# A decode kernel on one core: the tile context is closed behind the first three loads instead of around the whole program

## The chip, the cores and the metric

The kernel runs on 1 core of one Trainium2 chip. The metric is the device time of one execution in microseconds (us); less is better.

## The reference

One token (x, 512 values) goes through two branches, and a scalar gate mixes them. All numbers are float32.

```python
g = sigmoid((x * gate_w).sum(-1))
q = (x @ wq)                                  # 32 heads of 128
scores = q . k_cache * 128 ** -0.5            # 8 kv heads, 32768 positions, 4 query heads share one
a = softmax(scores) @ v_cache @ wo            # 4096 -> 512
b = (silu(x @ w1) * (x @ w3)) @ w2            # 512 -> 1792 -> 512
return g * a + (1 - g) * b
```

The K and V caches are 8 x 32768 x 128 floats each, 134 MB; with the weights the kernel reads 296 MB from HBM.

## The kernel before, in words

The program is written out by hand: it allocates its own semaphores (42 of them, in `_program`) and places every wait itself. The tile framework only wraps it. `kernel` opens a tile context at L485; `tile_gated_mix_decode_kernel` opens a critical section in it at L27, whose synchronizing engine is ScalarE (the profile's ACT), and runs the whole of `_program` inside. Instructions which the section emits at its entry and exit carry L27, those of the context L485. The start of every program, with four small constants and a barrier of all engines, carries L476.

Three SBUF buffers of 8 MB (64 KB in each of 128 partitions), ra, rb and rc, take all large loads. SyncE (SP in the profile) issues them, in this order: wq into rc (L118), w1 and w3 into the two parts of rb (L119, L120), then the two halves of the first K part into ra (L121, L122). Next it waits until the matmuls with w1 and w3 have freed rb (L123) and loads the second K part into rb (L124). Then a loop over the 8 kv heads loads each further half of K into ra or rb, and each half of V into rc, as TensorE releases the buffer (L127 to L137). At the end it loads the last V halves into ra and rb, wo into rc (L146) and w2 into ra (L152).

ScalarE issues three small transfers at the start: x (L155), the gate weights (L156) and, once VectorE has cleared a row, that zero row to the output (L162). At the end it issues the result (L460). Its semaphore l_out counts 16 for each of the two output transfers.

The work at the start: GpSimd (POOL) builds an identity and clears buffers (L166 to L173), VectorE (DVE) clears and reduces (L160 to L177), TensorE (PE) spreads x over the partitions (L187) and multiplies the gate (L196) as soon as x and the gate weights are there, then the query from wq (L202) and the two branches of the feed-forward from w1 and w3 (L229). ScalarE applies the sigmoids (L209, which needs a table load, and L241).

In the loop of 8 heads VectorE transposes K in 32 x 32 blocks (L342), TensorE multiplies (L271), VectorE and TensorE find the maxima, ScalarE exponentiates (L386), and TensorE multiplies with V of the head before (L285). Behind the loop come the last head, the projection with wo (L421), w2 (L428, L438), and four copies of a piece of the result each (L456). The program ends with GpSimd's wait for both output transfers (L461); then the section and the context are left.

Of the kernel before, what the change touches and what calls it, by code (L numbers as in the profile page):

```python
# [3 lines left out]
F32 = mybir.dt.float32  # L4
# [5 lines left out]
P = 128  # L10
# [13 lines left out]

@with_exitstack
def kernel(ctx, tc, x, k_cache, v_cache, wq, wo, w1, w3, w2, gate_w, out):
    with tc.tile_critical(sync_engine=mybir.EngineType.Activation, no_gpsimd_drain=True):  # L27
        _program(tc.nc, x, k_cache, v_cache, wq, wo, w1, w3, w2, gate_w, out)


def _program(nc, x, k_cache, v_cache, wq, wo, w1, w3, w2, gate_w, out):
    pe, dve, act, pool, sp = nc.tensor, nc.vector, nc.scalar, nc.gpsimd, nc.sync
    _, HKV, S, DH = k_cache.shape
    D = x.shape[-1]
    F = w1.shape[1]
    HQ = wq.shape[1] // DH
    REP = HQ // HKV
    NC = D // P
# [4 lines left out]
    W = NK * DH  # L43
    assert DH == P and D == 4 * P and REP == 4 and HKV == 8 and NK == 128 and F == FR * P

    def sb(name, *shape):
        return nc.alloc_sbuf_tensor(name, [P, *shape], F32).ap()

    def token(name):
        return nc.alloc_semaphore(name)  # L50

    def count(name):
        return Count(nc, name)


    ra, rb, rc = sb("ra", W), sb("rb", W), sb("rc", W)

    ident, ones, fold, dmask = sb("ident", P), sb("ones", P), sb("fold", 32), sb("dmask", 4)
    xp = sb("xp", NC, 32)
# [30 lines left out]
    pq = [bank(3), bank(4)]  # L90


    l_x, l_q = token("l_x"), token("l_q")
    l_a, l_a2, l_b, l_c = token("l_a"), token("l_a2"), token("l_b"), token("l_c")
    l_w1, l_w3 = token("l_w1"), token("l_w3")
    l_v = [token(f"l_v{i}") for i in range(2)]
    l_wo = [token(f"l_wo{i}") for i in range(2)]
    l_w2 = [token(f"l_w2{i}") for i in range(4)]
    l_out = token("l_out")

    c_q, c_k, c_v, c_e = (count(n) for n in ("c_q", "c_k", "c_v", "c_e"))
    c_nm, c_act, c_pool, done = token("c_nm"), count("c_act"), count("c_pool"), count("done")
# [12 lines left out]
    kd = k_cache.rearrange("a h (p m n) d -> (a h) m p (n d)", p=P, m=2, n=NK)  # L115
    vd = v_cache.rearrange("a h (r p n) d -> (a h) r p (n d)", r=2, p=P, n=NK)
    half = W // 2
    sp.dma_start(rc, wq.rearrange("(p c) n -> p (c n)", c=NC)).then_inc(l_q, 16)  # L118
    sp.dma_start(rb[:, 0:NC * F], w1.rearrange("(p c) f -> p (c f)", c=NC)).then_inc(l_w1, 16)  # L119
    sp.dma_start(rb[:, NC * F:2 * NC * F], w3.rearrange("(p c) f -> p (c f)", c=NC)).then_inc(l_w3, 16)  # L120
    sp.dma_start(ra[:, 0:half], kd[0, 0][:, 0:half]).then_inc(l_a, 16)  # L121
    sp.dma_start(ra[:, half:W], kd[0, 0][:, half:W]).then_inc(l_a2, 16)  # L122
    sp.wait_ge(c_e.sem, 2)  # L123
# [27 lines left out]
    for i in range(4):  # L151
# [17 lines left out]
        out=ident, in_=ident, compare_op=ALU.not_equal, fill=1.0, base=0, pattern=[[-1, P]], channel_multiplier=1,  # L169
# [256 lines left out]
    for k in range(W2[1]):  # L426
        t = k % 4
        i = pe.matmul(  # L428
            acc[32 * t:32 * t + 32, :], htp[:, k, :], w2t[:, k, :], start=False, stop=(k >= W2[1] - 4),
            skip_group_check=True,  # L430
        )
# [22 lines left out]
    for j in range(4):  # L454
        copy = act.copy if j % 2 else dve.tensor_copy
        i = copy(row[:, j * P:(j + 1) * P], pb[32 * j:32 * j + 1, 0:P])  # L456
# [1 line left out]
            done.by(i)  # L458
    act.wait_ge(done.sem, done.n)
    act.dma_start(od, row).then_inc(l_out, 16)  # L460
    c_pool.by(pool.wait_ge(l_out, 32))  # L461


# [26 lines left out]
```

## Time and profile before

| | us |
|---|---|
| runs shown | 693.97, 694.00, 694.11 |
| their median | 694.0 |
| the profiled execution's own time | 694.02 |
| its span, from the first to the last instruction | 691.9 |
| TensorE busy in the span | 368.2 |
| VectorE busy in the span | 307.0 |

The kernel moved 296.35 MB at a mean of 428 GB/s in the span.

How to read it: times in the profile count from the first instruction of the execution. "Busy" does not count register, branch, semaphore and DMA-issuing instructions; they belong to an engine's sequencer, which the rows mark with a q behind the engine (SPq, ACTq, POOLq, and PEldq for TensorE's). A row of the timeline has start, duration, engine, line, operation, what it writes and reads, and in brackets the idle time before it with what ended that. A row of a single source line has the count, the shortest, median and longest duration in ns, and the starts of the first and the last. "DMA to landing" is the time from issue to the arrival of the last byte. A row of the windows has the window, its length, the busy time of each engine with its instruction count (PE, PEld, DVE, ACT, POOL), the clock granted to TensorE, the mean share of the 16 DMA engines, and GB/s. The digits behind "DMA" on the page are that share in 40 equal slices of the span, in tenths.

### The profile page before, as it was taken

Reading aid. Unit: us, or ns where it says so; the run is one execution under the profiler, and the core shown is the slowest. Engines: PE = TensorE matmul, PEld = TensorE weight load, DVE = VectorE, ACT = ScalarE, POOL = GpSimd, SP = SyncE. Lnnn points to the kernel's source line nnn. Section 1 sums busy time; section 2 is a strip of 40 time slices with the busy share of each in tenths; the row PEclk is TensorE's granted clock in tenths of the full one; section 3 lists DMA queues with packets and bytes.
Section 4 is the critical chain, followed back from the end, with each engine's and each line's share of the span. In section 5 each row is a group of like instructions: output and inputs, shape, how many; then the busy total and the mean of one; then the engine's idle time right before and its main releaser. Section 6 shows DMA issues by size and latency. Waiting matters only on the chain. (4 is left out here: it accounts for less than half of the span.)

```text
span 691.9 us, 6738 instructions
## 1 busy us (share of the span) xinstructions
PE 368.2 (53%) x2952; PEld 107.5 (16%) x2952; DVE 307.0 (44%) x194; ACT 41.6 (6%) x111; POOL 7.0 (1%) x41
## 2 busy tenths in 40 slices
PE   1636255467463734466573735466463734466567
PEld 1100011103010121103010211103010211103122
DVE  1019378291725447091825446191816356181000
ACT  0020011002000010002000010001000010001000
POOL 0000000000000000000000000000000000000000
PEclk9975598868686977779577967888786966798678
DMA  9999999999999999999999999999999999999996
GB/s 383 421 439 454 424 429 425 447 447 424 425 432 432 436 447 436 424 424 432 432 440 451 428 424 428 436 428 443 447 424 424 432 432 436 447 436 424 424 423 291
DMA packets 6078, 296.35 MB, mean 428 GB/s; under 512 B 691, under 2 KB 691, under 8 KB 950
## 3 DMA queue, kind: packets, MB, share of 16 engines
q1 hardware_dynamic: 6048, 296.23, 99.2%
q8 instruction: 6, 0.10, 0.1%
q14 instruction: 2, 0.02, 0.0%
q10 hardware_dynamic: 22, 0.01, 0.0%
HBM read 296.23 MB, written 0.00 MB: 428 GB/s over the span
## 5 line engine op out<-in xcount | busy, mean ns | idle before, releaser
L342 DVE STREAM_TRANSPOSE rb<-rb 128x2048 f32<-128x2048 f32 x64 | 141.8, 2275 | 150.3 <-DVEq L112 150.3
L342 DVE STREAM_TRANSPOSE ra<-ra 128x2048 f32<-128x2048 f32 x64 | 141.4, 2275 | 43.6 <-DVEq L112 43.6
L271 PE MATMUL psum<-rb,winbuf 128*32 128x512 f32 x512 | 88.2, 766 | 130.2 <-PEq L112 130.2
L285 PE MATMUL psum<-rc,prob 128*32 128x512 f32 x896 | 111.2, 653 | 42.5 <-PEq L112 42.5
L271 PE MATMUL psum<-ra,winbuf 128*32 128x512 f32 x512 | 85.2, 764 | 86.7 <-PEq L112 86.7
L285 PEld LDWEIGHTS psum<-rc,prob 128*32 128x32 f32 x896 | 33.5, 120 | 115.5 <-issue 115.3
L366 DVE TENSOR_REDUCE mx<-psum 128x4 f32<-128x1024 f32 x8 | 9.8, 1224 | 81.6 <-DVEq L112 81.6
L271 PEld LDWEIGHTS psum<-rb,winbuf 128*32 128x32 f32 x512 | 13.1, 120 | 203.7 <-issue 203.7
L380 ACT COPY sbuf<-psum 128x512 f32<-128x512 f32 x16 | 9.8, 616 | 477.0 <-PE psum L271 477.0
L271 PEld LDWEIGHTS psum<-ra,winbuf 128*32 128x32 f32 x512 | 14.7, 121 | 150.1 <-issue 150.1
L386 ACT ACTIVATE prob<-psum,nm 128x256 f32<-128x256 f32 x32 | 18.8, 694 | 39.6 <-DVE nm L374 39.6
L295 PE MATMUL psum<-ident,sbuf 128*64 128x64 f32 x512 | 16.7, 223 | 0.8 <-PEq L112 0.8
L295 PEld LDWEIGHTS psum<-ident,sbuf 128*64 128x64 f32 x512 | 15.6, 138 | 7.6 <-issue 7.6
L347 DVE SCALAR_TENSOR_TENSOR otall<-psum,gate,recip 128x4 f32 (+1 forms) x8 | 1.7, 213 | 33.1 <-DVEq L112 33.1
L202 PE MATMUL psum<-rc,xp 128*32 128x512 f32 x64 | 9.8, 783 | 9.2 <-DMA rc<-in_A_wq_dram 9.2
L285 PE MATMUL psum<-rb,prob 128*32 128x512 f32 x64 | 8.4, 684 | 9.8 <-DMA rb<-in_A_v_cache_dram 9.8
L421 PE MATMUL psum<-rc,oq 128*32 128x512 f32 x64 | 10.7, 829 | 2.5 <-DMA rc<-in_A_wo_dram 2.1
L258 POOL COPY winbuf<-winraw 32x16 f32<-32x16 f32 x32 | 6.1, 189 | 537.2 <-PE psum L271 499.6
L285 PE MATMUL psum<-ra,prob 128*32 128x512 f32 x64 | 9.5, 761 | 3.7 <-DMA ra<-in_A_v_cache_dram 3.7
L229 PE MATMUL psum<-rb,xp 128*32 128x448 f32 x64 | 8.4, 683 | 5.6 <-DMA rb<-in_B_w_dram 5.6
L214 DVE STREAM_TRANSPOSE rc<-psum 128x512 f32<-128x512 f32 x2 | 1.3, 696 | 18.7 <-PE psum L202 18.7
L305 PE MATMUL psum<-fold,ob 128*128 128x4 f32 x64 | 8.4, 255 | 0.8 <-PEq L112 0.8
(62 smaller groups left out, 80.6 us busy)
## 6 DMA issues: line engine op xcount, KB each, us to landing
ra<-in_A_k_cache_dram SPq DMA_DIRECT2D x2, 4096.0 KB, 53.3
rc<-in_A_wo_dram SPq DMA_DIRECT2D x2, 4096.0 KB, 45.9
rb<-in_B_w_dram SPq DMA_DIRECT2D x2, 3584.0 KB, 34.7
ra<-in_B_w_dram SPq DMA_DIRECT2D x1, 1536.0 KB, 32.8
ra<-in_B_w_dram SPq DMA_DIRECT2D x1, 1024.0 KB, 35.0
ra<-in_B_w_dram SPq DMA_DIRECT2D x1, 768.0 KB, 36.3
ra<-in_B_w_dram SPq DMA_DIRECT2D x1, 256.0 KB, 36.5
rc<-in_A_v_cache_dram SPq DMA_DIRECT2D x14, 30.6
```

Of the source, the lines that this page charges most:

```text
L202: m = pe.matmul(pq[b][32 * j:32 * j + 32, :], xp[:, c, :], rc[:, o:o + REP * DH], start=(c == 0), stop=(c == NC - 1),)
L229: i = pe.matmul(ps[32 * j:32 * j + 32, 0:FJ], xp[:, c, :], rb[:, o:o + FJ], start=(c == 0), stop=(c == NC - 1))
L258: pool.tensor_copy(winbuf[32 * r:32 * r + 32, 16:144].rearrange("p (c k) -> p c k", k=32)[:, :, 4 * r:4 * r + REP], winraw[32 * r:32 * r + ...
L271: i = pe.matmul(s_ps[m][32 * g:32 * g + 32, :], winbuf[:, w:w + 32], region.rearrange("p (n c i) -> p c n i", c=4, i=32)[:, c, n:n + 16], ...
L285: i = pe.matmul(o_ps[32 * t:32 * t + 32, :], prob[:, w:w + 32], region[:, n * DH:(n + 4) * DH], start=(r == 0 and g == 0 and f == 0), stop ...
L295: i = pe.matmul(pf[64 * s:64 * s + 64, 64 * a:64 * a + 64], sbuf[:, a].rearrange("p i m -> p (i m)"), ident.rearrange("p (gf r s q) -> p s ...
L305: i = pe.matmul(mb[:, 0:REP], ob[:, b * P:(b + 1) * P], fold[:, 4 * b:4 * b + 4], start=(b == 0), stop=(b == 3))
L342: dve.transpose(part[:, c], part[:, c]).then_inc(t_tr, 1)
L366: dve.tensor_reduce(mx, pf.rearrange("p (a q) -> p q a", q=REP), axis=AX.X, op=ALU.max).then_inc(t_mx, 1)
L380: act.copy(sbuf[:, :, :, m], s_ps[m].rearrange("p (n i) -> p n i", i=32)).then_inc(t_ev, 1)
L386: act.activation(prob[:, 0:1024].rearrange("p (a n q) -> p n a q", a=16, q=REP)[:, :, :, q], pf.rearrange("p (n a q) -> p n a q", n=16, q= ...
L421: pe.matmul(acc[32 * t:32 * t + 32, :], oq[:, k:k + 32], rc[:, k * D:(k + 1) * D], start=(k < 4), stop=False, skip_group_check=True,)
```

## The change

`tile_gated_mix_decode_kernel` no longer opens a critical section. It allocates rb and rc and three semaphores, issues the loads of wq, w1 and w3 from SyncE inside the context, marked so that the framework puts no semaphores of its own on them, closes and compiles the context by hand, and then runs `_program`, which follows the context without a section. `_program` allocates only ra (behind rb and rc now), and its SyncE part begins with the first K part. At the end GpSimd still waits for both output transfers, and then clears all semaphores of the program. The `with` at L485 that opens the context is left as it is.

```diff
 def tile_gated_mix_decode_kernel(ctx, tc, x, k_cache, v_cache, wq, wo, w1, w3, w2, gate_w, out):
-    with tc.tile_critical(sync_engine=mybir.EngineType.Activation, no_gpsimd_drain=True):
-        _program(tc.nc, x, k_cache, v_cache, wq, wo, w1, w3, w2, gate_w, out)
-
-
-def _program(nc, x, k_cache, v_cache, wq, wo, w1, w3, w2, gate_w, out):
+    nc = tc.nc
+    rb, rc = (nc.alloc_sbuf_tensor(n, [P, 16384], F32).ap() for n in ("rb", "rc"))
+    l_q, l_w1, l_w3 = (nc.alloc_semaphore(n) for n in ("l_q", "l_w1", "l_w3"))
+    loads = [(rc, wq, l_q)]
+    n = w1.shape[0] * w1.shape[1] // P
+    loads += [(rb[:, i * n:(i + 1) * n], w, sem) for i, (w, sem) in enumerate(((w1, l_w1), (w3, l_w3)))]
+    for to, w, sem in loads:
+        i = nc.sync.dma_start(to, w.rearrange("(p c) n -> p (c n)", p=P)).then_inc(sem, 16)
+
+        tc.no_tile_sem_insts.add(i.ins.name)
+    tc.close()
+    tc.compile()
+    _program(nc, rb, rc, l_q, l_w1, l_w3, x, k_cache, v_cache, wq, wo, w1, w3, w2, gate_w, out)
+
+
+def _program(nc, rb, rc, l_q, l_w1, l_w3, x, k_cache, v_cache, wq, wo, w1, w3, w2, gate_w, out):
...
+    before = nc.snapshot_sems()
+
+
+    ra = sb("ra", W)
...
-    sp.dma_start(rc, wq.rearrange("(p c) n -> p (c n)", c=NC)).then_inc(l_q, 16)
-    sp.dma_start(rb[:, 0:NC * F], w1.rearrange("(p c) f -> p (c f)", c=NC)).then_inc(l_w1, 16)
-    sp.dma_start(rb[:, NC * F:2 * NC * F], w3.rearrange("(p c) f -> p (c f)", c=NC)).then_inc(l_w3, 16)
     sp.dma_start(ra[:, 0:half], kd[0, 0][:, 0:half]).then_inc(l_a, 16)
...
     act.dma_start(od, row).then_inc(l_out, 16)
-    c_pool.by(pool.wait_ge(l_out, 32))
+    pool.wait_ge(l_out, 32)
+    nc.clear_and_free_semaphores([l_q, l_w1, l_w3, *nc.allocated_since(before)])
```

More of the change, by code (lines that the diff above doesn't have):

```diff
@@ L53, in count @@
         return Count(nc, name)
-    ra, rb, rc = sb("ra", W), sb("rb", W), sb("rc", W)
+    before = nc.snapshot_sems()
+    ra = sb("ra", W)
     ident, ones, fold, dmask = sb("ident", P), sb("ones", P), sb("fold", 32), sb("dmask", 4)
@@ L90, in _program @@
     pq = [bank(3), bank(4)]
-    l_x, l_q = token("l_x"), token("l_q")
+    l_x = token("l_x")
     l_a, l_a2, l_b, l_c = token("l_a"), token("l_a2"), token("l_b"), token("l_c")
-    l_w1, l_w3 = token("l_w1"), token("l_w3")
     l_v = [token(f"l_v{i}") for i in range(2)]
```

## The prediction, made before the result was known

> **What bounds the kernel now.** I read the page first (span, slices, DMA queues), then the windows by stage, then the beginning and the end of the timeline, and last the rows of the lines that emit the section's own instructions (L27) and the context's (L485).
>
> ```profile
> span 691.9 us, 6738 instructions
> PE 368.2 (53%) x2952; PEld 107.5 (16%) x2952; DVE 307.0 (44%) x194; ACT 41.6 (6%) x111; POOL 7.0 (1%) x41
> DMA  9999999999999999999999999999999999999996
> q1 hardware_dynamic: 6048, 296.23, 99.2%
> 60.00:672.00 612.00, 327.30 (x2642) 94.33 (x2642) 290.96 (x173) 34.68 (x89) 5.30 (x28) 0.78 1.00 433
> ```
>
> The reader is to see that the 16 DMA engines are the bound: the q1 row gives their share by the SyncE queue's packets as 99.2% of the span, and in the window from 60 to 672 us the DMA share is 1.00. The busiest engine, TensorE, is at 53%. A change that touches no transfer can therefore act in three places only: when the stream starts, whether it ever runs dry, and what is left after its last byte.
>
> The beginning and the start of the loop:
>
> ```profile
> 0.92 0.37 SPq L118 DMA_DIRECT2D rc<-in_A_wq_dram  x1
> 0.97 0.53 ACTq L155 DMA_DIRECT2D ob<-in_A_x_dram  x1
> 1.54 0.73 ACTq L156 DMA_DIRECT2D prob<-in_gate_w_dram  x1
> 1.78 0.22 POOL L173 MEMSET winbuf<- 128x144 f32 x1
> 1.82 0.42 SPq L120 DMA_DIRECT2D rb<-in_B_w_dram  x1
> 2.08 0.27 DVE L177 TENSOR_REDUCE dmask<-ident 128x4 f32<-128x128 f32 x1
> 2.29 0.53 SPq L121 DMA_DIRECT2D ra<-in_A_k_cache_dram  x1
> 2.31 0.43 ACTq L162 DMA_DIRECT2D out_dram<-sbuf  x1
> 2.77 1.28 ACT L209 ACT_TABLE_LOAD   x1 [2.77 <-DVE ones L165]
> 10.74 1.94 PEld L187 LDWEIGHTS psum<-ones,ob 1*128 1x128 f32 x8 [10.74 <-DMA prob<-in_gate_w_dram]
> 13.11 0.55 PE L196 MATMUL psum<-gsm,ones 1*128 1x1 f32 x2 [0.35 <-PEq L112]
> 22.82 9.83 PE L202 MATMUL psum<-rc,xp 128*32 128x512 f32 x64 [9.15 <-DMA rc<-in_A_wq_dram]
> 46.64 0.33 SPq L124 DMA_DIRECT2D rb<-in_A_k_cache_dram  x1
> ```
>
> SyncE issues five loads within 2.5 us and then has nothing to do until 46.64, when both w matmuls have freed rb. TensorE waits 9.15 us for wq after all its small work is done. The head of the program is thus loose on every engine; only the first issue, at 0.92, is tight.
>
> The end, after the last matmul, with the rows of L27, L461 and L485 (count, ns of one, first to last start):
>
> ```profile
> 689.85 0.21 ACTq L460 DMA_DIRECT2D out_dram<-prob  x1
> L461 POOLq EVENT_SEMAPHORE  x1: 17/17/17, 691.0 to 691.0; - x1
> L27 POOLq NOP  x1: 13/13/13, 691.1 to 691.1; - x1
> L27 ACTq DRAIN  x1: 158/158/158, 690.2 to 690.2; - x1
> L485 POOLq DRAIN  x3: 34/41/64, 691.1 to 691.6; - x3
> L485 POOLq EVENT_SEMAPHORE  x4: 17/17/17, 691.2 to 691.7; - x4
> L485 POOLq EVENT_SEMAPHORE_RANGE_CLEAR  x1: 71/71/71, 691.5 to 691.5; - x1
> L485 SPq EVENT_SEMAPHORE  x4: 17/22/73, 690.2 to 691.8; - x4
> L485 DVEq EVENT_SEMAPHORE  x2: 21/21/21, 691.4 to 691.8; - x2
> L485 ACTq EVENT_SEMAPHORE  x2: 17/17/17, 691.4 to 691.8; - x2
> L485 PEldq EVENT_SEMAPHORE  x2: 51/51/51, 691.4 to 691.8; - x2
> ```
>
> GpSimd sees the landed result at 691.0 (L461). What follows, up to 691.9, computes nothing: GpSimd leaves the section (L27), gathers all engines, releases them at 691.4 (the first of the two that each of VectorE, ScalarE and TensorE has), clears a range of semaphores at 691.5 and releases all again at 691.8. That is 0.9 us, with rounding 0.8 to 0.9, on the path that sets the end. The profiled execution took 694.02 us, so 2.1 us lie around the span; it stands 0.02 above the median of the runs (694.0).
>
> **The change part by part.**
>
> *The tail.* Gone from the end are the exit from the section and the context's gathering, release, clearing, gathering and release. Added behind L461 is a clearing by GpSimd alone. I read it as the same range clear (71 ns), perhaps with one drain ahead (at most 64 ns). Nine GpSimd instructions lie from the NOP at 691.1 to the last release at 691.7, counting it and the three kinds of L485 rows: 1 + 3 + 4 + 1. They take some 0.08 us apiece, waits included. So: one step of 0.08 to the first new instruction, 0.071 for the clear, one more 0.08 if a drain stands ahead, together 0.15 to 0.25 us in place of 0.8 to 0.9. The gain is 0.55 to 0.75 us; I take 0.65. No other engine's end can come later: the last matter for ACT, the issue of the result, starts at 689.85, and its wait for all others is gone.
>
> *The first load.* These are the rows that stand between the start barrier and the first load:
>
> ```profile
> L476 SPq EVENT_SEMAPHORE  x1: 17/17/17, 0.7 to 0.7; - x1
> L485 SPq COMPARE_BRANCH  x1: 33/33/33, 0.8 to 0.8; - x1
> L27 ACTq NOP  x2: 14/16/18, 0.7 to 691.1; - x2
> ```
>
> SyncE is released by the start barrier at 0.7, branches at 0.8 when ScalarE's NOP of the section (0.7) has signalled, and issues at 0.92. In the changed kernel the loads stand in the context itself, so they don't wait for ScalarE. If the branch stays, only the handshake goes, which is under 0.1 us; if it goes too, the issue comes right behind the release, at about 0.7, 0.2 us earlier. Nothing suggests a later issue, so the bounds are 0 and 0.25 us. I take 0.1, since a branch into the context's block is likely to stay. The whole stream moves by this, and the end with it, since the window rows show no stretch in which another engine sets the pace.
>
> *What is moved to the head.* Behind the three loads every engine now goes through the closing sequence, 0.7 to 0.9 us by the rows of the tail. SyncE's third issue ends at 1.82 + 0.42 = 2.24 now, at 2.1 if all shifts by 0.1. So the program proper starts at about 2.9 to 3.0 us on all engines, where ScalarE and SyncE stood at 0.97 (L155) and 2.29 (L121). Queue by queue:
>
> - SyncE's two loads of the K cache (L121, L122) are issued 0.6 to 0.8 us later. They wait behind the three weight loads anyway:
>
> ```profile
> L120 SPq DMA_DIRECT2D rb<-in_B_w_dram x1: 424/424/424, 1.8 to 1.8; - x1
> DMA to landing us min/median/max: 39.4/39.4/39.4
> L121 SPq DMA_DIRECT2D ra<-in_A_k_cache_dram x1: 530/530/530, 2.3 to 2.3; - x1
> DMA to landing us min/median/max: 48.7/48.7/48.7
> L122 SPq DMA_DIRECT2D ra<-in_A_k_cache_dram x1: 521/521/521, 2.9 to 2.9; - x1
> DMA to landing us min/median/max: 57.8/57.8/57.8
> ```
>
>   The third load lands at 1.8 + 39.4 = 41.2, so the cover is some 36 us. Cost: nothing.
> - ScalarE's three small transfers (x, the gate weights, the zero row) are issued 2.0 us later. The gate weights release TensorE at 10.74, and TensorE is done with the small chain at 13.11 + 0.55 = 13.7, then waits 9.15 us. With 2.0 us more, and even with a few us more because the SyncE packets now all stand in front, it is done before 22.8. Cost: nothing; it would begin to cost beyond 9 us.
> - GpSimd's memsets (the last at 1.78), VectorE's reductions (2.08) and ScalarE's table load (2.77 + 1.28 = 4.05): all done by 4.1 us now, by 6.1 then, and used from 10.74 on at the earliest. Cost: nothing.
> - The later end of the chain: rb is asked for at 46.64 and the second half of ra lands at 2.9 + 57.8 = 60.7, so even a chain 10 us late would find the queue filled.
>
> *What stays.* The loop, its waits and all 6048 packets of q1 are as before. The three large buffers change places in SBUF; no row bears on that, and I cost it at nothing, with 0.2 us to either side for the scatter (the runs lie 0.14 us apart).
>
> **Sum.** 694.02 - 0.65 (tail) - 0.1 (first issue) = 693.27; against the median, 694.0 - 0.75 = 693.25. I predict **693.2 us**, 0.11% less. With the ends of the terms, 0.55 to 1.0 us of gain, and the scatter, this case's own range is 692.8 to 693.7.
>
> **One rule weighed.** The rows end at 691.9 and the time says 694.02; what the 2.1 us between are made of no row shows. The Trainium skill, page "Runtime: NRT & Kernel Launch", section "The ~15µs preamble/postamble breakdown", puts behind a kernel a wait for all engines and a reset of semaphores that each engine does. By that rule engines that come home early could do their share early, which is rival 3; if GpSimd's own share is the longest, the sum stays.
>
> **The rivals.**
>
> 1. *The clearing is done one by one* (slower). The diff names a list of semaphores, and the code allocates 42. If GpSimd took one instruction for each, at the 0.08 us per GpSimd instruction worked out above, it would be 3.4 us, all of it behind L461, where nothing covers it: -0.85 + 3.4 - 0.1 = +2.4, 696.5 us. It decides from 12 instructions on (0.95 / 0.08), and beyond 0.2% from some 30. Against it: the present clearing of the context is a single row, x1 at 71 ns. For it: no row shows what that one covers. Chance 7%.
>
> 2. *The closing at the head waits for the loads* (slower). If the drain held SyncE until the three loads have landed, the program would start at 41.2 + 0.7 = 42 us. The stream would be dry from about 41 until a new issue delivers, and the query and w matmuls (9.83 us for L202 alone) would come after 42 + some 4 us for the small chain, so rb would be asked for 15 to 20 us later than 46.64, against a slack of 60.7 - 46.6 = 14 us. Together 4 to 10 us: 697 to 703. Against it: ScalarE's drain of L27 at 690.2 took 158 ns, and ended 0.6 us before GpSimd saw the transfer which ScalarE itself had issued at 689.85. Chance 5%.
>
> 3. *The time around the span shrinks as well* (faster). TensorE, VectorE and ScalarE now all end at 691.8; then they would end by about 690.1, when the result is issued, 1.0 us ahead of GpSimd. If part of the 2.1 us is work of theirs, the time falls by up to 1.0 more: 692.2 to 693.0. For it: the 2.1 us are there. Against it: no row says whose they are. Chance 15%, of which 10 lie beyond 0.2%.
>
> 4. *The change doesn't do what it says*: the context's exit emits its closing sequence a second time at the end. Then the tail keeps its 0.8 and gains 0.15 for the clear: 694.02 + 0.15 - 0.1 = 694.1, no change. For it: L485 is the line of the context itself, which the diff doesn't touch. Against it: the diff closes and compiles the context by hand, and a second closing would have nothing to close. Chance 8%.
>
> **How the numbers follow.** Forecast 60%, rival 1 7%, rival 2 5%, rival 3 15%, rival 4 8%; 5% is left for something in the loop that the rows don't show, which I put on the slow side. A measurement of this kernel tells about 0.2% from no change, which is 1.4 us, so the bounds are 692.6 and 695.4. Faster beyond: 11% (rival 3 and an edge of the forecast). Slower beyond: 7 + 5 + 3 = 15%. Within: 74%. The range that should hold the time 8 times in 10 takes in the forecast, most of rival 3 and rival 4: 692.4 to 694.2.
>
> **What would show it.** In the changed profile: the first issue of wq at 0.7 to 0.9; the drains and releases of the context's line and one range clear at 2 to 3 us instead of 691 to 692; ScalarE's load of x at about 3; TensorE still waiting for wq, for 5 to 8 us instead of 9.15; the span ending 0.15 to 0.25 us after GpSimd's wait for the result; q1's 6048 packets in a stream of the same length. Wrong would be: a TensorE that no longer waits for wq, a DMA digit under 9 in the second or third slice, a row of dozens of semaphore instructions on GpSimd at the end, or a difference between time and span that isn't 2.1 us.

## The result

| | before | changed |
|---|---|---|
| median of 22 runs each | 694.01 us | 693.01 us |
| lowest to highest | 693.76 to 694.21 | 692.85 to 693.36 |
| profiled execution, its own time | 694.02 us | 692.93 us |
| its span | 691.9 us | 691.1 us |
| what lies around the span | 2.17 us | 1.84 us |

The ratio is 0.9986, with a 95% interval of 0.998 to 0.9992: about 1 us faster, and just outside "no difference". The forecast was 693.2.

"What lies around the span" is the profiled execution's own time less its span, here by the spans before rounding, 691.85 and 691.09 us. The prediction's 2.1 was worked out from the rounded 691.9.

The page of the changed kernel, its span, DMA slices and q1 row:

```profile
span 691.1 us, 6720 instructions
DMA  9999999999999999999999999999999999999997
q1 hardware_dynamic: 6048, 296.23, 99.2%
```

The bound is what it was: the same 6048 packets, the same share. All that moved lies ahead of the stream and behind it. The head of the changed kernel, by the timeline:

```profile
0.73 0.37 SPq L34 DMA_DIRECT2D rc<-in_A_wq_dram  x1
1.16 0.90 SPq L34 DMA_DIRECT2D rb<-in_B_w_dram  x2
2.84 0.33 SPq L130 DMA_DIRECT2D ra<-in_A_k_cache_dram  x1
2.85 0.52 ACTq L164 DMA_DIRECT2D ob<-in_A_x_dram  x1
3.42 0.73 ACTq L165 DMA_DIRECT2D prob<-in_gate_w_dram  x1
15.19 2.02 PE L196 MATMUL psum<-ones,ob 1*128 1x1 f32 x8 [15.19 <-DMA prob<-in_gate_w_dram]
17.57 0.55 PE L205 MATMUL psum<-gsm,ones 1*128 1x1 f32 x2 [0.35 <-PEq L124]
22.66 8.92 PE L211 MATMUL psum<-rc,xp 128*32 128x512 f32 x64 [4.54 <-DMA rc<-in_A_wq_dram]
40.94 6.15 PE L238 MATMUL psum<-rb,xp 128*32 128x448 f32 x32 [6.36 <-DMA rb<-in_B_w_dram]
47.16 0.33 SPq L133 DMA_DIRECT2D rb<-in_A_k_cache_dram  x1
```

The first load is issued at 0.73 instead of 0.92. The program proper starts at 2.84 (the first K part, the load of x), and the gate weights release TensorE at 15.19 instead of 10.74, but TensorE still waits 4.54 us for wq.

Two groups of sequencer rows of the changed kernel: the closing of the context (L38) and GpSimd's end (L471).

```profile
L38 POOLq EVENT_SEMAPHORE  x4: 17/17/17, 2.3 to 2.7; - x4
L38 SPq DRAIN  x3: 7/7/123, 2.1 to 2.5; - x3
L38 SPq EVENT_SEMAPHORE  x2: 17/17/17, 2.4 to 2.8; - x2
...
L471 POOLq DRAIN  x1: 111/111/111, 690.7 to 690.7; - x1
L471 POOLq EVENT_SEMAPHORE_RANGE_CLEAR  x1: 266/266/266, 690.8 to 690.8; - x1
```

The closing sequence now stands between 2.1 and 2.8 us, under the first loads. There is no range clear in it. The end is two rows on GpSimd: a drain, which carries the wait for the result, from 690.7, and one clear from 690.8, which takes 266 ns where the context's clear of before took 71.

### The profile page after: what moved, and what is told of

It reads as the page before. It is cut to its first block, busy times and chain, and to the rows that moved or that the text cites. A ratio compares the mean times of both kernels' runs of the same rounds, so it can differ in the third digit from the quotient of the medians.

```text
span 691.1 us, 6720 instructions
## 1 busy us (share of the span) xinstructions
PE 369.2 (53%) x2952; PEld 107.3 (16%) x2952; DVE 307.0 (44%) x194; ACT 41.7 (6%) x111; POOL 7.1 (1%) x41
## 3 DMA queue, kind: packets, MB, share of 16 engines
q1 hardware_dynamic: 6048, 296.23, 99.2%
## 5 line engine op out<-in xcount | busy, mean ns | idle before, releaser
L280 PE MATMUL psum<-rb,winbuf 128*32 128x512 f32 x512 | 91.1, 790 | 126.4 <-PEq L124 126.4
L294 PE MATMUL psum<-rc,prob 128*32 128x512 f32 x896 | 115.3, 672 | 41.3 <-PEq L124 41.3
L280 PE MATMUL psum<-ra,winbuf 128*32 128x512 f32 x512 | 82.2, 739 | 88.1 <-PEq L124 88.1
L238 PE MATMUL psum<-rb,xp 128*32 128x448 f32 x64 | 9.3, 743 | 6.4 <-DMA rb<-in_B_w_dram 6.4
L196 PE MATMUL psum<-ones,ob 1*128 1x1 f32 x8 | 2.0, 370 | 15.2 <-DMA prob<-in_gate_w_dram 15.2
L430 PE MATMUL psum<-rc,oq 128*32 128x512 f32 x64 | 7.3, 595 | 3.5 <-DMA rc<-in_A_wo_dram 3.1
```

The costliest lines, as they stand in the source:

```text
L238: i = pe.matmul(ps[32 * j:32 * j + 32, 0:FJ], xp[:, c, :], rb[:, o:o + FJ], start=(c == 0), stop=(c == NC - 1))
L280: i = pe.matmul(s_ps[m][32 * g:32 * g + 32, :], winbuf[:, w:w + 32], region.rearrange("p (n c i) -> p c n i", c=4, i=32)[:, c, n:n + 16], ...
L294: i = pe.matmul(o_ps[32 * t:32 * t + 32, :], prob[:, w:w + 32], region[:, n * DH:(n + 4) * DH], start=(r == 0 and g == 0 and f == 0), stop ...
L430: pe.matmul(acc[32 * t:32 * t + 32, :], oq[:, k:k + 32], rc[:, k * D:(k + 1) * D], start=(k < 4), stop=False, skip_group_check=True,)
```

## The experiments

All times are medians of 9 to 12 runs, ratios are to runs of the kernel before on the same chip; those have medians of 693.98 to 694.06 us. The span and what lies around it are those of the profiled execution. Over all runs of a kernel the median of time less span is within 0.06 us of its profiled value, so one execution can stand for its kernel here. A gathering of all engines means that each engine drains and signals, and then waits until GpSimd releases all of them.

**The head without the new end.** The changed kernel gets back two gatherings of all engines around its clear.

```diff
     pool.wait_ge(l_out, 32)
+    nc.all_engine_barrier()
     nc.clear_and_free_semaphores([l_q, l_w1, l_w3, *nc.allocated_since(before)])
+    nc.all_engine_barrier()
```

> The head of the change with an end like that of before: behind GpSimd's wait a gathering of all engines, the clear, and a second gathering. Theory: the head alone is worth its 0.19 us (first issue 0.92 to 0.73), and the end costs what it cost before plus the longer clear (266 ns instead of 71), so the span is 690.7 + 0.9 + 0.2 = 691.8 us. The time around the span, which went from 2.1 to 1.8 us with the change, belongs to engines that end together with GpSimd, so it comes back to 2.1: 693.9 us. Rival: that 0.3 us is not tied to the end; then 1.8 us lie around the span and the time is 693.6 us.

Measured: 693.60 us, ratio 0.999 (0.998 to 1.0001), span 691.7, 1.9 us around it. The sequencer rows of the first gathering and of the second, on GpSimd:

```profile
L471 POOLq EVENT_SEMAPHORE  x2: 17/17/17, 690.8 to 690.9; - x2
...
L473 POOLq EVENT_SEMAPHORE  x2: 17/17/17, 691.5 to 691.6; - x2
```

The span is as expected, and the new end is worth 693.60 - 693.01 = 0.6 us. With an end as long as that of before and a clear 0.2 us longer, the kernel is still 0.4 us ahead, of which the head's 0.19 is a part; 0.2 more is the time around the span, which came back to 1.9 only, against 2.2 before. So this run speaks rather for the rival.

**One gathering at the end.**

```diff
     nc.clear_and_free_semaphores([l_q, l_w1, l_w3, *nc.allocated_since(before)])
+    nc.all_engine_barrier()
```

> The changed kernel with one gathering of all engines behind its clear. Both theories: the span grows by one gathering, some 0.35 us, to 691.4. Theory that the time around the span depends on whether all engines end together: 2.1 us around it, 693.6 us. Rival, that it doesn't: 1.8 us around it, 693.3 us.

Measured: 693.66 us, ratio 0.9991 (0.9981 to 1.0001), span 691.5, 2.2 us around it. This one speaks for the theory: what lies around its span is what lies around that of the kernel before (2.17 us in both). Its span is 0.2 us shorter than that of the run before, and its time is not. The two together settle nothing about the time around the span, except that it isn't constant.

**The cover of the closing sequence taken away.** The context is closed ahead of the three loads.

```diff
-    loads = [(rc, wq, l_q)]
-    n = w1.shape[0] * w1.shape[1] // P
-    loads += [(rb[:, i * n:(i + 1) * n], w, sem) for i, (w, sem) in enumerate(((w1, l_w1), (w3, l_w3)))]
-    for to, w, sem in loads:
-        i = nc.sync.dma_start(to, w.rearrange("(p c) n -> p (c n)", p=P)).then_inc(sem, 16)
-
-        tc.no_tile_sem_insts.add(i.ins.name)
     tc.close()
     tc.compile()
...
+    sp.dma_start(rc, wq.rearrange("(p c) n -> p (c n)", c=NC)).then_inc(l_q, 16)
+    sp.dma_start(rb[:, 0:NC * F], w1.rearrange("(p c) f -> p (c f)", c=NC)).then_inc(l_w1, 16)
+    sp.dma_start(rb[:, NC * F:2 * NC * F], w3.rearrange("(p c) f -> p (c f)", c=NC)).then_inc(l_w3, 16)
     sp.dma_start(ra[:, 0:half], kd[0, 0][:, 0:half]).then_inc(l_a, 16)
```

> The context is closed ahead of the three loads instead of behind them, so the closing sequence loses its cover. Theory: the first issue comes some 0.7 us later than in the changed kernel, at 1.4 us, and the whole stream with it: span 691.8, time 693.7 us. Rival, that the stream makes up for a late start: 693.0 us.

Measured: 693.83 us, ratio 0.9992 (0.9982 to 1.0003), span 691.8. The timeline has the first issue, and the sequencer rows the end:

```profile
1.38 0.37 SPq L123 DMA_DIRECT2D rc<-in_A_wq_dram  x1
...
L467 POOLq DRAIN  x1: 111/111/111, 691.4 to 691.4; - x1
```

The first issue comes 0.65 us later than in the changed kernel (1.38 against 0.73), GpSimd sees the result 0.7 later (691.4 against 690.7), and the time is 0.8 us longer. A later start of the stream moves the end by about as much. Issuing the loads ahead of the closing is what makes the closing free; without that cover hardly anything of the change's gain is left.

**The small chain later, by VectorE.** Six more clearings by VectorE hold back ScalarE's load of x.

```diff
+    slow = count("slow")
+    for _ in range(6):
+        dve.wait_ge(slow.sem, slow.n)
+        slow.by(dve.memset(flat[:, 0:1024], 0.0))
+    act.wait_ge(slow.sem, slow.n)
     act.dma_start(xr, x.rearrange("a b d -> (a b) d")).then_inc(l_x, 16)
...
     local = count("local")
+    dve.wait_ge(slow.sem, slow.n)
     n_zero = local.by(dve.memset(zero, 0.0))
```

> The changed kernel with six more clearings of a 128 x 1024 buffer by VectorE, one after the other, ahead of ScalarE's load of x, which waits for them: all three small transfers and TensorE's small chain come some 6 to 8 us later. In the changed kernel TensorE still waits 4.5 us for wq. Theory: the chain now comes 2 to 4 us behind wq, and that costs nothing, because rb is asked for some 14 us before the queue needs it: 693.0 us. Rival, that the wait for wq is all the cover there is: 695 to 697 us.

Measured: 693.11 us, ratio 0.9987 (0.9977 to 0.9997). TensorE and SyncE in its timeline:

```profile
25.36 8.42 PE L217 MATMUL psum<-rc,xp 128*32 128x512 f32 x64
45.74 0.33 SPq L133 DMA_DIRECT2D rb<-in_A_k_cache_dram  x1
```

The query starts 2.7 us late (25.36 against 22.66) and rb is not asked for any later than before. The wait for wq is not the last cover.

**The small chain later, by wq.**

```diff
+    act.wait_ge(l_q, 16)
     act.dma_start(xr, x.rearrange("a b d -> (a b) d")).then_inc(l_x, 16)
```

> The changed kernel with ScalarE's load of x held until wq has landed, at 22.6 us instead of 2.9: the gate weights then land 10 to 12 us later, at 33 to 35, and the query starts at 36 to 38 us, some 14 us late. Theory: rb is asked for at about 60 instead of 46, at the limit of its 14 us, and VectorE's first blocks of K are 8 to 10 us late; the stream runs dry for a few us in the first head, and the time is 695 to 700 us. Rival, that the whole delay shows: 707 us; that the loop makes up for it: 693.0.

Measured: 693.12 us, ratio 0.9987 (0.9978 to 0.9997). My theory's 695 to 700 was wrong.

```profile
33.67 9.49 PE L212 MATMUL psum<-rc,xp 128*32 128x512 f32 x64
42.99 6.19 PE L239 MATMUL psum<-rb,xp 128*32 128x448 f32 x64
49.24 0.33 SPq L133 DMA_DIRECT2D rb<-in_A_k_cache_dram  x1
```

The query starts 11 us late, and rb is asked for at 49.24, only 2.1 us later than in the changed kernel. There TensorE had waited another 6.36 us for w3, until 40.94 (L238 above); here its matmuls on w1 and w3 run in one go from 42.99. The landing of w3 is a second cover behind the landing of wq, and I had added the matmuls up as if it were not there. The stream doesn't notice. The kernel before has the same wait, and the prediction, which counted on the 9.15 us ahead of the query alone, did not look at it:

```profile
41.30 5.27 PE L229 MATMUL psum<-rb,xp 128*32 128x448 f32 x32 [5.64 <-DMA rb<-in_B_w_dram]
```

**A longer clear.** 84 semaphores more, which nothing uses, stand in the range that is cleared.

```diff
     before = nc.snapshot_sems()
+    [nc.alloc_semaphore(f"pad{i}") for i in range(84)]
```

> The changed kernel with 84 more semaphores allocated, so that the clear at the end covers 126 instead of 42. Theory: a range clear costs by its length, (266 - 71) / (42 - 6) = 5.4 ns for each semaphore, so it takes 0.72 us instead of 0.27, and the time is 693.5 us. Rival: 266 ns is what a first clear costs at any length; 693.0.

Measured: 693.61 us, ratio 0.9995 (0.9986 to 1.0005), span 691.6.

```profile
L472 POOLq DRAIN  x1: 233/233/233, 690.6 to 690.6; - x1
L472 POOLq EVENT_SEMAPHORE_RANGE_CLEAR  x1: 721/721/721, 690.9 to 690.9; - x1
```

The clear takes 721 ns for 126 semaphores against 266 for 42: (721 - 266) / 84 = 5.4 ns for each, the figure expected. The drain ahead of it, 233 ns instead of 111, grows too, which the theory had not. Together the two rows take 0.58 us more, and the time is 0.6 us longer.

**The clear moved ahead of the last wait.** GpSimd clears all but two semaphores as soon as ScalarE has passed its wait for the result's last copies, while the result is still being written. Its last instruction waits for the result and subtracts its own 32.

```diff
-    d_s = token("d_s")
+    d_s, fin = token("d_s"), token("fin")
...
-    act.wait_ge(done.sem, done.n)
+    act.wait_ge(done.sem, done.n).then_inc(fin, 1)
     act.dma_start(od, row).then_inc(l_out, 16)
-    pool.wait_ge(l_out, 32)
-    nc.clear_and_free_semaphores([l_q, l_w1, l_w3, *nc.allocated_since(before)])
+    take(fin, 1, pool)
+    kept = (l_out.num, fin.num)
+    nc.clear_and_free_semaphores([l_q, l_w1, l_w3, *(s for s in nc.allocated_since(before) if getattr(s, "num", s) not in kept)])
+    take(l_out, 32, pool)
```

> The changed kernel with the clear of all semaphores but two moved ahead of GpSimd's wait for the result, into the time in which the result lands, and with a wait that subtracts its own 32 as the last instruction. Theory: drain and clear stand on the path one to one, so the 0.4 us between GpSimd's wait and the end of the span go, and the span ends at 690.7: 692.6 us. Rival: the drain and the clear overlap with what follows the span, and the time stays at 693.0.

Measured: 692.93 us, ratio 0.9981 (0.997 to 0.9991), span 690.7, 2.0 us around it.

```profile
L472 POOLq DRAIN  x3: 65/78/83, 689.6 to 690.1; - x3
L472 POOLq EVENT_SEMAPHORE_RANGE_CLEAR  x3: 88/113/118, 689.7 to 690.2; - x3
...
L124 POOLq EVENT_SEMAPHORE  x2: 17/17/17, 689.5 to 690.6; - x2
```

All clears start by 690.2, and GpSimd's last wait at 690.6 ends this execution's span 0.4 us earlier, as expected. But this was the fastest of the 12 executions (692.70 us); the median of their spans is 690.9, against 691.1 in the changed kernel. The median time fell by only 0.08 us, because 0.15 us more lie around the span (2.01 against 1.86 us, medians of all runs). So the gain of the span is real and more than half of it is given back outside, which neither theory had said. Here GpSimd's last instruction is a wait and no longer a clear; whether that is the reason no run shows.

**Another engine does the last wait.** The same kernel, with the last line on TensorE, SyncE, ScalarE or VectorE.

```diff
-    take(l_out, 32, pool)
+    take(l_out, 32, pe)   # or sp, act, dve
```

> As the kernel that clears ahead of the last wait, but TensorE does the last wait instead of GpSimd. Span as there, 690.7. Theory that the time around the span depends on which engines end late: it changes from what it is with GpSimd last, by 0.2 us or more, towards the 2.1 us of before. Rival: the same time as with GpSimd last, 692.6 us, since only the last end counts.

> As the kernel that clears ahead of the last wait, with SyncE doing the last wait. GpSimd last gave 692.93 us with 2.03 around a span of 690.67, TensorE last 692.64 with 1.74 around 690.93. Theory that the time around the span is longer by some 0.3 us when GpSimd ends last: with SyncE last it is as with TensorE, 692.6 us. Rival, that it varies with the program by 0.2 us for reasons not tied to the last engine: anything from 692.5 to 692.9.

> The same with ScalarE doing the last wait. Theory that GpSimd is the dear one: 692.6 us. Rival, that it is TensorE that is cheap: 692.9.

> The same with VectorE doing the last wait. Theory that GpSimd is the dear one: 692.6 us. Rival, that it is TensorE that is cheap: 692.9.

| last to end | time | ratio (95%) | span | around it (profiled) |
|---|---|---|---|---|
| GpSimd | 692.93 | 0.9981 (0.997 to 0.9991) | 690.7 | 2.0 |
| TensorE | 692.64 | 0.998 (0.9971 to 0.999) | 690.9 | 1.7 |
| SyncE | 692.36 | 0.9976 (0.9966 to 0.9985) | 690.9 | 1.5 |
| ScalarE | 692.40 | 0.9976 (0.9967 to 0.9985) | 690.8 | 1.6 |
| VectorE | 692.33 | 0.9975 (0.9965 to 0.9985) | 690.8 | 1.5 |

SyncE's kernel, the rows of the last wait and of GpSimd's clears:

```profile
L124 SPq EVENT_SEMAPHORE  x1: 17/17/17, 690.8 to 690.8; - x1
...
L472 POOLq DRAIN  x3: 65/78/83, 689.8 to 690.3; - x3
L472 POOLq EVENT_SEMAPHORE_RANGE_CLEAR  x3: 88/112/117, 689.9 to 690.4; - x3
```

GpSimd is done 0.4 us before the end here, and though the span is no shorter than with GpSimd last, the time is 0.6 us less (692.36 against 692.93). The three other engines agree within 0.1 us; TensorE lies between. So GpSimd is the dear one, and my theory's 692.6 for the three was 0.2 to 0.3 us too high. For TensorE the theory had the direction wrong: the time around the span fell to 1.7 us instead of rising towards that of before.

The kernels ran on three chips, but that is not the reason: the kernel before has 2.2 us around its span on each of them, and the next kernel, with GpSimd last, has 1.9 on the chip of the last three rows.

How much the other engines cost is not shown, only a limit. The profiled time less the end of GpSimd's last instruction is 1.87, 2.00 and 1.90 us with SyncE, ScalarE and VectorE last, and 1.84 to 1.97 in the six kernels whose span GpSimd's clear ends. So in the three, GpSimd's own end may still set the time, with the other engine's wait covered. With TensorE last it is 2.20, so TensorE would set the end there.

The kernels with SyncE, ScalarE or VectorE last beat both the one before and the changed one: 692.33 to 692.40 against 693.01 and 694.01.

**The code moved.** 40 waits more on each engine at the head.

```diff
+    for _ in range(40):
+        sp.wait_ge(l_x, 32)
     sp.wait_ge(c_e.sem, 2)
...
+    for engine in (pe, dve, act, pool):
+        for _ in range(40):
+            engine.wait_ge(l_x, 32)
     pe.wait_ge(l_x, 32)
```

> The changed kernel with 40 more waits on x on each engine, where TensorE, SyncE and the others have several us to spare, so that all later code stands 40 instructions further on. Theory: nothing but the cover at the head changes, and the time stays at 693.0 us. Rival, that the place of the code sets part of the 2 us around the span: a change of 0.1 to 0.3 us either way with the same span of 691.1.

Measured: 693.12 us, ratio 0.9987 (0.9978 to 0.9996), span 691.2, 1.9 us around it. That is 0.11 us above the changed kernel's 693.01, and most of it lies in the span: the time around it is 1.90 us against 1.86 (medians of all runs). By this shift at least, the place of the code does not move the time around the span by the 0.2 to 0.3 us in question.

## Why the prediction was right, step by step

The number was right to 0.2 us, with some luck: inside the span the terms erred in both directions and cancelled, and what the forecast missed lies around the span. Measured in the two profiled executions, 694.02 to 692.93, which is 1.09 us:

| step | forecast | measured | from |
|---|---|---|---|
| first load issued earlier | 0.1 | 0.19 | 0.92 to 0.73 |
| length of the stream, first issue to GpSimd's wait | 0 | 0.11 | 690.05 to 689.95 |
| the tail, GpSimd's wait to the end of the span | 0.65 | 0.47 | 0.88 to 0.41 |
| around the span | 0 | 0.32 | 2.17 to 1.84 |

The span fell by 0.77 us, where the forecast had 0.75.

*The first load.* "I take 0.1, since a branch into the context's block is likely to stay" was the wrong choice inside right bounds. SyncE issues right behind the start barrier.

*The stream.* The 0.11 is taken for scatter: in the other kernels with the same first issue, GpSimd sees the result between 690.6 and 690.9 us, and the forecast allowed 0.2.

*The tail.* The mechanism was right and a size was off. The step "I read it as the same range clear (71 ns)" failed. It is one range clear, but of more semaphores. Neither row says what it covers, but the longer clear gives the rate, 5.4 ns for each semaphore, and the changed program clears its 42. By that rate 71 ns, 195 ns less, is a clear of 36 fewer, which makes six; and the instructions of the critical section (L27) use six semaphores in the trace. The closing at the head of the changed kernel, where there is no section, has no clear at all, although the prediction expected one there. The drain, put at "at most 64 ns", has 111. Rival 1 asked what the old row covers, and that was the right question; with the answer, the tail's gain would have come out at 0.65 - 0.19 = 0.46.

*What was moved to the head.* Costs nothing, as forecast, and by more than forecast. The gate weights were issued 1.9 us later (1.54 to 3.42), near the 2.0 of the forecast, but released TensorE 4.45 us later (10.74 to 15.19). The forecast had left "a few us more" for that, though its 5 to 8 us of waiting for wq became 4.54; the cover was 9.15, and the two kernels with a late x show a second cover behind it.

*Rival 2*, a closing that waits for the loads, is refuted by one row: SyncE's longest drain of L38 takes 123 ns, and the whole closing is over by 2.8 us, with 38 us to go until the third load has landed.

*Rival 4* is refuted by the end of the changed kernel, where no row of the context stands.

*Rival 3*, that the time around the span shrinks, had 15% and came about in part: 0.32 of the 1.09 us. The prediction itself had named "a difference between time and span that isn't 2.1 us" as a sign of being wrong, and on that point it was. The Trainium skill (page "Runtime: NRT & Kernel Launch", section "The ~15µs preamble/postamble breakdown") puts a wait for all engines and then a reset of semaphores on each engine behind a kernel. That an engine which comes home early does its share early is the prediction's reading; the section doesn't say it. The runs with another engine last are in line with that reading: with GpSimd home 0.4 to 0.5 us before the end, 1.5 to 1.7 us lie around the span instead of 2.0. No run shows what the share consists of.

Open: why 2.2 us lie around the span of the kernel with one gathering and 1.9 around that with two, although in both all engines end together. Engine by engine the ends don't account for this 0.2 us: the last releases follow each other alike in both. So the cause of the 0.32 us is not settled; that GpSimd's end weighs more than that of the others is shown only where the last wait was moved.

## What to carry to other kernels

Where transfers bound a kernel, look at what stands ahead of the first issue and behind the last landing: a framework's opening and closing are worth moving under the stream, where the closing cost nothing here. A range clear was paid by the semaphore; if it must be done, do it while the last transfer lands, and let an engine other than GpSimd do the last wait. Price an instruction by what it covers, and not only by the name that its row shares with the new one, and compare the time with the span, since a gain of the one need not be a gain of the other.

## What was not expected of the hardware

- With GpSimd's last instruction at the end, 1.8 to 2.0 us lay around the span, in seven kernels; with SyncE, ScalarE or VectorE last and GpSimd done earlier, 1.5 to 1.6.
- 2 KB of gate weights, issued by ScalarE at 1.54, 3.42 or 23.24 us while SyncE's large loads were under way, released TensorE at 10.74, 15.19 and 30.81: 9.2, 11.8 and 7.6 us for a transfer that could hardly be smaller. The two rows of the late one, issue and release:

```profile
23.24 0.73 ACTq L166 DMA_DIRECT2D prob<-in_gate_w_dram  x1
30.81 2.02 PE L197 MATMUL psum<-ones,ob 1*128 1x1 f32 x8 [30.81 <-DMA prob<-in_gate_w_dram]
```
